# Turning the last batch's q with a transposing transfer, in a new order of all units

## The chip, the cores and the metric

The kernel runs on one core of one Trainium2 chip. The metric is the device time of one execution in microseconds (us); lower is better. The core has five engines with an instruction queue each: TensorE (PE; its weight loads are listed as PEld), VectorE (DVE), ScalarE (ACT), GpSimd (POOL) and SyncE (SP), which here only starts transfers. Sixteen DMA engines serve all queues.

## The reference

The inputs are q, k and v of shape (4 batches, 8 heads, 768 tokens, 64), a small matrix `sort_net` of 8 x 8 for each batch and head, and the weights of a gated layer. All are float32.

```
for _ in range(5):                       # P = sort_net, over 8 blocks of 96 tokens
    P = exp(P - max(P)); P /= rowsum(P); P /= colsum(P)
k_sorted, v_sorted = P @ k_blocks, P @ v_blocks           # blocks mixed by P
attn = softmax(q_block @ k_sorted_block.T / 8)            # 96 x 96 in each block
x = (attn @ v_sorted_block), heads side by side           # (4, 768, 512)

h = relu(x @ w_in);  u, v = h[:, :512], h[:, 512:]
v_n = (v - mean) / sqrt(var + 1e-6)
out = (u * (w_spatial @ v_n + b_spatial)) @ w_out         # (4, 768, 512)
```

## The kernel before

The kernel is written as units, small functions that each put a few instructions on one or two engines. The string `ORDER` (lines 18 to 51) names all units with their arguments, and the program calls them in that order; there is no scheduler behind it. Each engine works through its own instructions in the order in which the units issued them, and semaphores make it wait for what it reads and for the buffers it overwrites. So the order of the string decides everything. Most units that use TensorE begin with a number 0 to 3, the PSUM buffer (`ps0` to `ps3`, 4 KB per partition each) that takes the product; a letter A (ScalarE), D (VectorE) or P (GpSimd) names the engine that does the unit's copy or elementwise step. A PSUM buffer is free for the next unit when that copy has read it.

The units, with the line of their main instruction:

- Loads: `L:q:b`, `L:k:b`, `L:v:b` load one batch on GpSimd's queue, converting to bfloat16 (768 KB each); `L:wv`, `L:wu` are the halves of w_in, `L:wsa`, `L:wsb` those of w_spatial, `L:wo` is w_out. `LH` loads half of batch 0's q as float32 on SP, `QC` converts it. The tiles of q, k and v, of w_spatial and of the output come from one pool of eight, so a load can wait for a tile to come free.
- `DM` are filler products of a zero tile (L226), `SK` is one round of normalizing `sort_net` on ScalarE and VectorE, `PR` (L256) spreads the result over partitions, `P0`, `PC` and `PD` make from it the mixing matrices `pd` (batch 0 on VectorE, the others on GpSimd).
- q: `QT` and `QQ` turn the q of one or two pairs of heads, so that the head dimension lies on partitions, by products with the identity (L314: 12 or 24 of them), and copy the result from PSUM into `qT`. There are four pairs of heads in a batch.
- k: `KT` (L383) mixes the blocks of k and turns them in one product, and copies them into `kt_all` (six slots).
- v: batch 0 by `VT` (L383) and `VB` (L401); other batches by `VM` (L410) into the tile `vm`, which `VC` (L423, four transfers each on SP) rearranges into `vb`.
- Attention for a pair of heads and half of the blocks: `SC` (L442) makes the scores and ScalarE their exponentials (L447, five slots); `AT` (L488) multiplies them with v, and VectorE divides by the sums (L495, L496), giving `x_sb`.
- `XT` (L518) turns x by products with the identity in batches 0 and 1. In batches 2 and 3 `XD` does it with a transposing transfer on SP (L506, `dma_start_transpose`, 96 x 2048 elements).
- `VP` (L554; two tiles of 128 tokens, or one) makes the second half of h and `UP` (L597) the first. `ST` (L571, L572), `LN` and `LA` (L583) normalize the second half. `WW` (L531) turns w_spatial.
- `SP` (L609) multiplies with w_spatial, and VectorE adds the bias, giving `z` (L615, three tiles); `GT` (L626) multiplies z and u on VectorE or GpSimd, giving `gt`; `OP` (L635) multiplies with w_out. With a last argument 2 an `OP` does its 512 columns in two halves, 16 products of 256 columns in place of 8 of 512. `OE` (L115, L117) copies the result out of PSUM, `OS` stores it from SP's queue.
- The last batch uses finer units after a branch on a flag (`CK`, `CF`, `LF`): `SH`, `GH`, `OH` (L685), `OI` and `OJ` (L697), the last of which stores on SP's (S) or ScalarE's (A) queue.

In the old order every q is turned on TensorE: four `QT` in batch 0 and two `QQ` in each of batches 1, 2 and 3. Two units that the old order doesn't call are in the code all the same. `QP` (line 357) copies one pair of heads of q within SBUF into a tile `qp`, so that the two heads of a pair lie side by side. `QX` (line 368) turns all of it in one transposing transfer on SP:

```
        nc.sync.dma_start_transpose(
            out=q_tile(b)[:, lo * S:hi * S].rearrange("p (x c) -> p x c", c=128),
            in_=st["qp", b][:, lo:hi].rearrange("p k g h d -> p (k g h d)"),
        )
```

Of the kernel before, what the change touches and what calls it, by code (L numbers as in the profile page):

```python
# [15 lines left out]


ORDER = """
IV:0 CO S0 SK:0 SK:1 LH:S:0 L:q:0:4:8 L:k:0:0:8 L:v:0:0:8 SK:2 IV:2 ID MA L:v:1:0:8 MC QC:A:1 SK:3 L:k:1:0:8 MB QC:A:0
DM:0:6:512 L:q:1:0:8 DM:2:6:512 DM:1:6:512 QT:3:A:0:1 SK:4 QT:2:A:0:3 DM:0:6:512 DM:3:6:512 L:wv QT:1:A:0:0 QT:2:A:0:2  # L20
PR:0 P0:0:2 L:wu P0:6:8 P0:2:4 DM:3:6:512 P0:4:6 PC:D KT:1:D:0:1 PD:1:4:8 KT:3:A:0:0 L:wsb L:wsa KT:0:D:0:3 KT:2:A:0:2
IV:1 L:v:2:0:8 VT:1:A:0:0 VT:3:D:0:1 PD:1:0:4 SC:0:0:0:0 SC:2:0:0:1 VB:1:D:0:0 L:k:2:0:8 VB:3:D:0:1 SC:0:0:1:0
VT:1:A:0:2 AT:2:0:0:0 VT:3:A:0:3 PD:2:4:8 AT:0:0:1:0 L:q:2:0:8 VM:1:A:1:0 VB:2:D:0:2 SC:3:0:1:1 XT:0:D:0:0:0
AT:1:0:0:1 SC:2:0:2:0 VM:3:A:1:3 VB:0:D:0:3 PD:2:0:4 SC:1:0:2:1 AT:2:0:2:0 KT:3:D:1:1 KT:0:D:1:2 SC:1:0:3:0 VM:2:A:1:1
SC:3:0:3:1 AT:1:0:1:1 KT:2:A:1:3 KT:0:A:1:0 AT:3:0:3:0 VM:1:A:1:2 PD:3:4:8 QQ:2:D:1:0 XT:3:D:0:1:0 L:k:3:0:8
AT:0:0:3:1 XT:1:A:0:0:2 QQ:2:A:1:2 AT:3:0:2:1 VP:1:A:0:0:1 XT:0:D:0:1:2 ST:0:1 VP:2:D:0:2 ST:0:0 SC:0:1:1:1 SC:3:1:2:1
L:q:3:0:8 VC:1:4:8 VP:1:D:0:4:5 SC:2:1:3:1 ST:0:4 ST:0:5 SC:3:1:3:0 VP:0:A:0:3 SC:2:1:0:1 ST:0:2 UP:1:A:0:1:1
AT:0:1:1:1 L:v:3:0:8 SC:3:1:0:0 ST:0:3 UP:2:A:0:0:0 AT:0:1:3:1 AT:1:1:2:1 LN:0:0:6 UP:3:A:0:0:1 AT:0:1:0:1 LA:0:5
WW:2:A:0 WW:1:D:4 XT:3:A:1:1:2 UP:0:A:0:1:0 LA:0:2 VC:1:0:4 AT:2:1:0:0 VM:1:A:2:1 BI WW:3:D:2 SC:0:1:2:0 VM:2:A:2:2
XT:1:D:1:1:0 LA:0:0 BH LA:0:4 LA:0:1 LA:0:3 VM:3:A:2:0 SC:0:1:1:0 VP:1:A:1:4:5 AT:2:1:3:0 AT:0:1:1:0 ST:1:5 SP:3:0:2  # L30
AT:0:1:2:0 L:wo SP:1:0:0 VM:2:D:2:3 SP:0:0:1 VC:2:4:8 XT:3:D:1:0:2 XT:1:A:1:0:0 VC:2:0:4 QQ:2:D:2:0 KT:0:A:2:1
KT:3:D:2:0 GT:D:0:0 QQ:1:D:2:2 KT:2:A:2:2 KT:0:A:2:3 PD:3:0:4 GT:P:0:2 VP:3:A:1:0:1 SC:1:2:0:1 SC:2:2:0:0 SP:0:0:3
ST:1:4 SC:3:2:2:1 SC:1:2:1:1 ST:1:1 VP:2:A:1:2:3 KT:3:D:3:2 QQ:0:D:3:0 ST:1:2 SC:1:2:3:0 UP:2:A:1:1:0 AT:0:2:0:1
GT:P:0:3 KT:3:A:3:0 ST:1:3 QQ:1:D:3:2 SC:0:2:3:1 AT:2:2:2:1 UP:3:D:1:0:1 VM:1:A:3:3 UP:0:A:1:0:0 AT:2:2:3:1
UP:3:A:1:1:1 GT:P:0:1 ST:1:0 LN:1:0:6 AT:2:2:1:1 AT:0:2:3:0 XD:2:1 LA:1:4 OP:1:0:0:2 AT:2:2:0:0 OE:A:0:0 OP:0:0:2:2
SC:2:2:2:0 LA:1:2 LA:1:5 OE:D:0:2 SC:1:2:1:0 LA:1:1 LA:1:0 LA:1:3 OP:3:0:4:2 AT:1:2:1:0 AT:0:2:2:0 SP:2:1:2 VM:0:D:3:1
VM:1:D:3:0 OE:A:0:4 VP:3:D:2:4:5 KT:0:A:3:1 KT:2:D:3:3 SP:1:1:3 VM:0:A:3:2 GT:D:1:3 OS:0:0 ST:2:4 SP:3:1:1 SC:2:3:3:1
SC:1:3:1:1 XD:2:0 OS:0:2 GT:D:1:2 ST:2:5 SP:0:1:0 VC:3:4:8 SC:3:3:2:1 SC:2:3:0:1 UP:1:D:2:1:0 GT:D:1:1 VC:3:0:4
VP:3:A:2:2:3 AT:1:3:3:1 GT:P:1:0 VP:2:A:2:0:1 ST:2:3 AT:1:3:2:1 AT:3:3:1:1 UP:0:A:2:1:1 OP:1:1:0 ST:2:0 ST:2:1 ST:2:2
OE:A:1:0 AT:2:3:0:1 LN:2:0:6 LA:2:1 UP:0:D:2:0:0 SC:1:3:0:0 LA:2:3 SC:3:3:1:0 LA:2:2 LA:2:5 LA:2:0 OP:2:1:4 AT:1:3:0:0  # L40
AT:3:3:1:0 XD:3:1 OE:A:1:4 OP:0:1:2 LA:2:4 SC:1:3:3:0 OE:D:1:2 SC:3:3:2:0 SP:2:2:2 AT:1:3:2:0 UP:0:A:2:0:1 AT:3:3:3:0
CK VP:2:A:3:4:5 GT:D:2:2 OS:1:2 SP:1:2:1 ST:3:5 OS:1:4 XD:3:0 SP:3:2:3 SP:2:2:0 ST:3:4 CF:3 GT:D:2:1 GT:P:2:3
UP:0:A:3:1:0 VP:2:D:3:2:3 VP:3:A:3:0:1 ST:3:0 ST:3:1 ST:3:2 UP:2:A:3:0:1 GT:P:2:0 LF OP:1:2:2 ST:3:3 OE:A:2:2 LN:3:0:6
OP:0:2:0 LA:3:4 LA:3:5 OS:2:2 OE:A:2:0 UP:3:D:3:1:1 LA:3:2 LA:3:0 OP:2:2:4 LA:3:3 OE:A:2:4 LA:3:1 OS:2:4 UP:0:A:3:0:0
SH:1:3:3:0 GH:P:3:3:0 SH:2:3:0:0 GH:D:3:0:0 SH:0:3:1:0 SH:2:3:2:0 SH:3:3:1:1 GH:P:3:1:0 SH:1:3:0:1 GH:P:3:2:0 OS:1:0
GH:P:3:1:1 SH:2:3:3:1 SH:3:3:2:1 OS:2:0 GH:P:3:0:1 GH:D:3:2:1 GH:D:3:3:1 OS:0:4 IF OH:1:3:2:0:512:0:4
OH:2:3:3:0:512:0:4 OH:0:3:4:0:256:0:4 OI:A:3:2:0:512 OI:A:3:3:0:512 OH:3:3:5:0:256:0:4 OI:D:3:4:0:256 OI:D:3:5:0:256
OJ:3:2:0:512:S OJ:3:3:0:512:S OJ:3:4:0:256:S OJ:3:5:0:256:A OH:2:3:5:256:512:0:4 OH:1:3:1:0:512:0:4
OH:3:3:4:256:512:0:4 OI:D:3:5:256:512 OI:A:3:1:0:512 OJ:3:5:256:512:S OI:A:3:4:256:512 OJ:3:4:256:512:S OJ:3:1:0:512:A
OH:2:3:0:0:512:0:4 OI:A:3:0:0:512 OJ:3:0:0:512:S  # L50
"""


# [773 lines left out]
```

## Time and profile before

| | |
|---|---|
| median of 3 runs | 156.73 us (156.33 to 156.81) |
| the profiled execution: time, span | 156.77 us, 155.0 us |
| PE busy | 148.5 us (96% of the span) |
| DVE busy | 120.3 us (78%) |
| ACT busy | 81.6 us (53%) |
| POOL busy | 36.8 us (24%) |
| DMA, share of 16 engines | software queue (POOL) 48.0%, hardware queue (SP) 25.4% |
| loaded from HBM, written to it | 24.78 MB, 6.29 MB |

The span runs from the first to the last instruction that the profiler saw; the execution's own time holds 1.77 us more. Busy shares are averages over stages. Of the chain of work that ended last 93% of the span are PE's. A line of the chain reads start, length, engine, line and count; a line of the timeline reads start, length, engine, line, what is written and read, count and, in brackets, the idle time ahead of it with what ended it.

### The profile page before, as it was taken

Reading aid. Unit: us, or ns where it says so; the run is one execution under the profiler, and the core shown is the slowest. Engines: PE = TensorE matmul, PEld = TensorE weight load, DVE = VectorE, ACT = ScalarE, POOL = GpSimd, SP = SyncE. Lnnn points to the kernel's source line nnn. Section 1 sums busy time; section 2 is a strip of 40 time slices with the busy share of each in tenths; the row PEclk is TensorE's granted clock in tenths of the full one; section 3 lists DMA queues with packets and bytes.
Section 4 is the critical chain, followed back from the end, with each engine's and each line's share of the span. In section 5 each row is a group of like instructions: output and inputs, shape, how many; then the busy total and the mean of one; then the engine's idle time right before and its main releaser. Section 6 shows DMA issues by size and latency. Waiting matters only on the chain.

```text
span 155.0 us, 4028 instructions
## 1 busy us (share of the span) xinstructions
PE 148.5 (96%) x1689; PEld 92.1 (59%) x1689; DVE 120.3 (78%) x261; ACT 81.6 (53%) x112; POOL 36.8 (24%) x43
## 2 busy tenths in 40 slices
...
GB/s 72 267 203 204 205 204 205 208 217 238 271 217 203 203 204 204 242 226 16 0 17 224 43 198 64 147 1 4 102 148 185 44 0 0 131 49 371 141 226 183
DMA packets 27653, 23.57 MB, mean 152 GB/s; under 512 B 7280, under 2 KB 24688, under 8 KB 27632
## 3 DMA queue, kind: packets, MB, share of 16 engines
q0 software_dynamic: 14352, 11.80, 48.0%
q1 hardware_dynamic: 12992, 11.10, 25.4%
...
q8 instruction: 14, 0.23, 0.6%
...
HBM read 24.78 MB, written 6.29 MB: 201 GB/s over the span
## 4 chain that ended last, share of the span: by engine, by line
PE 93%; ACT 3%; DVE 1%; issue 1%; DVEq 0%; ACTq 0%
PE ps L609 15%; PE ps L554 14%; PE ps L597 14%; PE ps L635 10%; PE ps L226 7%; PE ps L488 5%; PE ps L665 5%; PE ps L442 4%; PE ps L383 4%; PE ps L314 4%; PE ps L685 3%; PE ps L410 2%; PE ps L518 2%; PE ps L531 1%; PE ps L401 1%; ACT kt_all L115 1%
## 5 line engine op out<-in xcount | busy, mean ns | idle before, releaser
L447 ACT ACTIVATE ex_all<-ps 96x768 bf16<-96x768 f32 x32 | 24.8, 805 | 8.7 <-PE ps L442 8.6
L626 POOL TENSOR_TENSOR gt<-z,u_sb 128x768 bf16<-128x768 f32 x6 | 9.8, 1642 | 78.6 <-DVE z L615 61.3
L609 PE MATMUL ps<-wspT,v_sb 128*128 128x384 bf16 x144 | 25.1, 326 | 0.0
L597 PE MATMUL ps<-xT,w_in_sb 128*128 128x384 bf16 x128 | 23.5, 326 | 0.0
L554 PE MATMUL ps<-w_in_sb,xT 128*128 128x512 bf16 x96 | 22.9, 380 | 0.2 <-issue 0.2
L496 DVE TENSOR_TENSOR x_sb<-ps,rec_all 96x512 bf16<-96x512 f32 x32 | 22.0, 687 | 1.1
L609 PEld LDWEIGHTS <-v_sb 128*128 128x128 bf16 x144 | 13.5, 98 | 8.9
L571 DVE BATCH_NORM_STATS2 stats<-v_sb 128x6 f32<-128x512 bf16 x24 | 16.3, 678 | 2.0 <-ACT v_sb L121 1.5
L115 ACT COPY o_sb<-ps 128x1024 f32<-128x1024 f32 (+2 forms) x12 | 9.7, 816 | 15.2 <-PE ps L685 10.2
L635 PE MATMUL ps<-w_out_sb,gt 128*128 128x256 bf16 (+1 forms) x96 | 16.9, 326 | 0.0
L615 DVE TENSOR_TENSOR z<-ps,b_bc 128x768 f32<-128x768 f32 x12 | 11.4, 952 | 7.0 <-PE ps L609 6.8
L121 ACT ACTIVATE u_sb<-ps 128x768 bf16<-128x768 f32 x12 | 9.7, 810 | 13.1 <-PE ps L597 13.0
L597 PEld LDWEIGHTS <-w_in_sb 128*128 128x128 bf16 x128 | 11.6, 98 | 7.4
L554 PEld LDWEIGHTS <-xT 128*128 128x128 bf16 x96 | 8.6, 98 | 9.7 <-issue 0.7
L121 ACT ACTIVATE v_sb<-ps 128x1024 bf16<-128x1024 f32 (+1 forms) x9 | 8.8, 976 | 9.1 <-PE ps L554 9.1
L488 PEld LDWEIGHTS <-ex_all 96*128 96x128 bf16 x256 | 10.6, 97 | 3.7 <-issue 0.6
L488 PE MATMUL ps<-vb,ex_all 96*128 96x65 bf16 x256 | 12.2, 193 | 0.5 <-issue 0.5
L635 PEld LDWEIGHTS <-gt 128*128 128x128 bf16 x96 | 9.0, 98 | 5.5
L226 PE MATMUL ps<-warm 128*128 128x512 bf16 x36 | 10.7, 461 | 1.3 <-DVE warm L201 1.3
L115 ACT CAST kt_all<-ps 128x768 bf16<-128x768 f32 x9 | 6.9, 800 | 6.5 <-PE ps L383 6.5
L442 PE MATMUL ps<-qT,kt_all 64*128 64x96 bf16 x256 | 9.3, 204 | 0.4 <-DVE kt_all L117 0.4
L495 DVE RECIPROCAL rec_all<-ps 96x8 f32<-96x8 f32 x32 | 6.3, 196 | 4.3 <-PE ps L488 4.0
...
## 6 DMA issues: line engine op xcount, KB each, us to landing
...
k_in<-in_k_dram POOLq DMA_DIRECT2D x4, 768.0 KB, 23.2
v_in<-in_v_dram POOLq DMA_DIRECT2D x4, 768.0 KB, 22.3
vb<-vm SPq DMA_DIRECT2D x24, 99.0 KB, 5.8
q_in<-in_q_dram POOLq DMA_DIRECT2D x3, 768.0 KB, 29.8
...
q<-in_q_dram SPq DMA_DIRECT2D x1, 768.0 KB, 4.6
```

The source lines that it names most:

```text
L115: nc.scalar.copy(out=out, in_=in_)
L121: nc.scalar.activation(out=out, in_=in_, func=AF.Relu)
L226: nc.tensor.matmul(t[:, 0, 0:int(w)], lhsT=warm[:, 0:128], rhs=warm[:, 0:int(w)], start=True, stop=True)
L442: nc.tensor.matmul(t[:, hh, 0:HW].rearrange("p (g x) -> p g x", g=G)[:, :, ii * TB:(ii + 1) * TB], lhsT=kT[rows, i * BLK:i * BLK + 128], r ...
L447: nc.scalar.activation(out=e_tile(b, hp, ih).rearrange("p h (x g) -> p h x g", g=G), in_=t[0:BLK, :, 0:HW].rearrange("p h (g x) -> p h x g ...
L488: nc.tensor.matmul(t[:, hh, ii * VW:ii * VW + D + 1], lhsT=e[:, c:c + 128], rhs=vb[b % 2][:, ih * NI + ii, 2 * hp + hh, 0:D + 1], start=Tr ...
L496: nc.vector.tensor_mul(out=x_sb[:, hp].rearrange("p i (h d) -> p h i d", h=2), in0=tv[:, :, :, 0:D], in1=_raw_ap(rec, 0, [rec.ap[0], [NI, ...
L554: nc.tensor.matmul(t[:, x, :], lhsT=st["xT", b][:, n // 3, kc, (n % 3) * 128:(n % 3 + 1) * 128], rhs=w_in_sb[:, kc, DH:DFF], start=(kc == ...
L571: nc.vector.bn_stats(out=stats, in_=st["v_sb", b, n])
L597: nc.tensor.matmul(t[:, x, 0:HW], lhsT=w_in_sb[:, kc, mc * 128:(mc + 1) * 128], rhs=st["xT", b][:, ih, kc, :], start=(kc == 0), stop=(kc = ...
L609: nc.tensor.matmul(t[:, x, 0:HW], lhsT=st["v_sb", b, n][:, mc * 128:(mc + 1) * 128], rhs=wspT[:, 3 * x:3 * x + 3, n, :], start=(n == 0), s ...
L635: nc.tensor.matmul(t[:, x, c:c + w], lhsT=st["gt", b, mc][:, (n0 + x) * 128:(n0 + x + 1) * 128], rhs=w_out_sb[:, mc, c:c + w], start=(mc = ...
```

## The change

The string `ORDER` is replaced; no function changes. The new string differs in four ways:

- Batch 3 has no `QQ`. Four `QP` (three on ScalarE, one on VectorE) and one `QX:3:0:4` take their place: 128 x 3072 elements in one transposing transfer on SP, behind the `VC` of batch 2 and ahead of the first `XD`.
- All other units are the same in number, but nearly all stand at other places, use other PSUM buffers, and in part copy on another engine. Batch 0's first loads are v, k, half of q (before: half of q, k, v), those of batch 1 v, q, k (before: v, k, q), those of batch 3 q, v, k. The order holds 62 changes between products of different shape (64 columns, 64 rows, full), where the old one holds 65.
- All nine `OP` of batches 0 to 2 are done in two halves; before, only the three of batch 0.
- In the tail the products, copies and stores come in another order: the last `OH` has 256 columns and is copied by VectorE (before: 512 columns, ScalarE), and four of its eight stores go out on ScalarE's queue (before: two of eight). The last two entries of the list are both stores, `OJ:3:4:0:256:A` ahead of `OJ:3:5:256:512:S`, exchanged against the order in which their copies stand.

```diff
 ORDER = """
-IV:0 CO S0 SK:0 SK:1 LH:S:0 L:q:0:4:8 L:k:0:0:8 L:v:0:0:8 SK:2 IV:2 ID MA L:v:1:0:8 MC QC:A:1 SK:3 L:k:1:0:8 MB QC:A:0
-DM:0:6:512 L:q:1:0:8 DM:2:6:512 DM:1:6:512 QT:3:A:0:1 SK:4 QT:2:A:0:3 DM:0:6:512 DM:3:6:512 L:wv QT:1:A:0:0 QT:2:A:0:2
-PR:0 P0:0:2 L:wu P0:6:8 P0:2:4 DM:3:6:512 P0:4:6 PC:D KT:1:D:0:1 PD:1:4:8 KT:3:A:0:0 L:wsb L:wsa KT:0:D:0:3 KT:2:A:0:2
-IV:1 L:v:2:0:8 VT:1:A:0:0 VT:3:D:0:1 PD:1:0:4 SC:0:0:0:0 SC:2:0:0:1 VB:1:D:0:0 L:k:2:0:8 VB:3:D:0:1 SC:0:0:1:0
-VT:1:A:0:2 AT:2:0:0:0 VT:3:A:0:3 PD:2:4:8 AT:0:0:1:0 L:q:2:0:8 VM:1:A:1:0 VB:2:D:0:2 SC:3:0:1:1 XT:0:D:0:0:0
-AT:1:0:0:1 SC:2:0:2:0 VM:3:A:1:3 VB:0:D:0:3 PD:2:0:4 SC:1:0:2:1 AT:2:0:2:0 KT:3:D:1:1 KT:0:D:1:2 SC:1:0:3:0 VM:2:A:1:1
-SC:3:0:3:1 AT:1:0:1:1 KT:2:A:1:3 KT:0:A:1:0 AT:3:0:3:0 VM:1:A:1:2 PD:3:4:8 QQ:2:D:1:0 XT:3:D:0:1:0 L:k:3:0:8
-AT:0:0:3:1 XT:1:A:0:0:2 QQ:2:A:1:2 AT:3:0:2:1 VP:1:A:0:0:1 XT:0:D:0:1:2 ST:0:1 VP:2:D:0:2 ST:0:0 SC:0:1:1:1 SC:3:1:2:1
-L:q:3:0:8 VC:1:4:8 VP:1:D:0:4:5 SC:2:1:3:1 ST:0:4 ST:0:5 SC:3:1:3:0 VP:0:A:0:3 SC:2:1:0:1 ST:0:2 UP:1:A:0:1:1
-AT:0:1:1:1 L:v:3:0:8 SC:3:1:0:0 ST:0:3 UP:2:A:0:0:0 AT:0:1:3:1 AT:1:1:2:1 LN:0:0:6 UP:3:A:0:0:1 AT:0:1:0:1 LA:0:5
-WW:2:A:0 WW:1:D:4 XT:3:A:1:1:2 UP:0:A:0:1:0 LA:0:2 VC:1:0:4 AT:2:1:0:0 VM:1:A:2:1 BI WW:3:D:2 SC:0:1:2:0 VM:2:A:2:2
-XT:1:D:1:1:0 LA:0:0 BH LA:0:4 LA:0:1 LA:0:3 VM:3:A:2:0 SC:0:1:1:0 VP:1:A:1:4:5 AT:2:1:3:0 AT:0:1:1:0 ST:1:5 SP:3:0:2
-AT:0:1:2:0 L:wo SP:1:0:0 VM:2:D:2:3 SP:0:0:1 VC:2:4:8 XT:3:D:1:0:2 XT:1:A:1:0:0 VC:2:0:4 QQ:2:D:2:0 KT:0:A:2:1
-KT:3:D:2:0 GT:D:0:0 QQ:1:D:2:2 KT:2:A:2:2 KT:0:A:2:3 PD:3:0:4 GT:P:0:2 VP:3:A:1:0:1 SC:1:2:0:1 SC:2:2:0:0 SP:0:0:3
-ST:1:4 SC:3:2:2:1 SC:1:2:1:1 ST:1:1 VP:2:A:1:2:3 KT:3:D:3:2 QQ:0:D:3:0 ST:1:2 SC:1:2:3:0 UP:2:A:1:1:0 AT:0:2:0:1
-GT:P:0:3 KT:3:A:3:0 ST:1:3 QQ:1:D:3:2 SC:0:2:3:1 AT:2:2:2:1 UP:3:D:1:0:1 VM:1:A:3:3 UP:0:A:1:0:0 AT:2:2:3:1
-UP:3:A:1:1:1 GT:P:0:1 ST:1:0 LN:1:0:6 AT:2:2:1:1 AT:0:2:3:0 XD:2:1 LA:1:4 OP:1:0:0:2 AT:2:2:0:0 OE:A:0:0 OP:0:0:2:2
-SC:2:2:2:0 LA:1:2 LA:1:5 OE:D:0:2 SC:1:2:1:0 LA:1:1 LA:1:0 LA:1:3 OP:3:0:4:2 AT:1:2:1:0 AT:0:2:2:0 SP:2:1:2 VM:0:D:3:1
-VM:1:D:3:0 OE:A:0:4 VP:3:D:2:4:5 KT:0:A:3:1 KT:2:D:3:3 SP:1:1:3 VM:0:A:3:2 GT:D:1:3 OS:0:0 ST:2:4 SP:3:1:1 SC:2:3:3:1
-SC:1:3:1:1 XD:2:0 OS:0:2 GT:D:1:2 ST:2:5 SP:0:1:0 VC:3:4:8 SC:3:3:2:1 SC:2:3:0:1 UP:1:D:2:1:0 GT:D:1:1 VC:3:0:4
-VP:3:A:2:2:3 AT:1:3:3:1 GT:P:1:0 VP:2:A:2:0:1 ST:2:3 AT:1:3:2:1 AT:3:3:1:1 UP:0:A:2:1:1 OP:1:1:0 ST:2:0 ST:2:1 ST:2:2
-OE:A:1:0 AT:2:3:0:1 LN:2:0:6 LA:2:1 UP:0:D:2:0:0 SC:1:3:0:0 LA:2:3 SC:3:3:1:0 LA:2:2 LA:2:5 LA:2:0 OP:2:1:4 AT:1:3:0:0
-AT:3:3:1:0 XD:3:1 OE:A:1:4 OP:0:1:2 LA:2:4 SC:1:3:3:0 OE:D:1:2 SC:3:3:2:0 SP:2:2:2 AT:1:3:2:0 UP:0:A:2:0:1 AT:3:3:3:0
-CK VP:2:A:3:4:5 GT:D:2:2 OS:1:2 SP:1:2:1 ST:3:5 OS:1:4 XD:3:0 SP:3:2:3 SP:2:2:0 ST:3:4 CF:3 GT:D:2:1 GT:P:2:3
-UP:0:A:3:1:0 VP:2:D:3:2:3 VP:3:A:3:0:1 ST:3:0 ST:3:1 ST:3:2 UP:2:A:3:0:1 GT:P:2:0 LF OP:1:2:2 ST:3:3 OE:A:2:2 LN:3:0:6
-OP:0:2:0 LA:3:4 LA:3:5 OS:2:2 OE:A:2:0 UP:3:D:3:1:1 LA:3:2 LA:3:0 OP:2:2:4 LA:3:3 OE:A:2:4 LA:3:1 OS:2:4 UP:0:A:3:0:0
-SH:1:3:3:0 GH:P:3:3:0 SH:2:3:0:0 GH:D:3:0:0 SH:0:3:1:0 SH:2:3:2:0 SH:3:3:1:1 GH:P:3:1:0 SH:1:3:0:1 GH:P:3:2:0 OS:1:0
-GH:P:3:1:1 SH:2:3:3:1 SH:3:3:2:1 OS:2:0 GH:P:3:0:1 GH:D:3:2:1 GH:D:3:3:1 OS:0:4 IF OH:1:3:2:0:512:0:4
-OH:2:3:3:0:512:0:4 OH:0:3:4:0:256:0:4 OI:A:3:2:0:512 OI:A:3:3:0:512 OH:3:3:5:0:256:0:4 OI:D:3:4:0:256 OI:D:3:5:0:256
-OJ:3:2:0:512:S OJ:3:3:0:512:S OJ:3:4:0:256:S OJ:3:5:0:256:A OH:2:3:5:256:512:0:4 OH:1:3:1:0:512:0:4
-OH:3:3:4:256:512:0:4 OI:D:3:5:256:512 OI:A:3:1:0:512 OJ:3:5:256:512:S OI:A:3:4:256:512 OJ:3:4:256:512:S OJ:3:1:0:512:A
-OH:2:3:0:0:512:0:4 OI:A:3:0:0:512 OJ:3:0:0:512:S
+S0 CO SK:0 BH LH:S:0 IV:2 L:v:0:0:8 SK:1 SK:2 ID MA L:k:0:0:8 L:q:0:4:8 DM:3:6:512 DM:0:6:512 L:v:1:0:8 L:q:1:0:8
+QC:A:0 SK:3 QC:A:1 MB SK:4 DM:2:6:512 DM:1:6:512 MC QT:2:D:0:1 DM:1:6:512 DM:3:6:512 PR:1 L:k:1:0:8 QT:2:A:0:0 P0:0:2
+L:wv L:wsb P0:4:6 P0:6:8 IV:0 P0:2:4 PC:D VT:0:A:0:0 KT:3:D:0:0 L:wu PD:1:0:4 VT:2:A:0:1 L:v:2:0:8 KT:1:A:0:3
+KT:0:D:0:2 SC:2:0:0:1 VB:3:D:0:0 PD:1:4:8 KT:1:A:0:1 QT:0:D:0:2 IV:1 QT:2:A:0:3 VB:3:D:0:1 SC:0:0:1:0 VT:1:D:0:3
+VT:2:A:0:2 L:wsa L:q:2:0:8 SC:3:0:0:0 PD:3:0:4 PD:3:4:8 AT:0:0:0:1 L:k:2:0:8 VB:1:D:0:3 SC:2:0:1:1 AT:3:0:0:0
+VM:0:A:1:0 VB:1:D:0:2 SC:2:0:2:0 AT:3:0:1:0 SC:0:0:3:0 AT:1:0:2:0 SC:2:0:2:1 AT:3:0:1:1 VM:0:A:1:2 AT:2:0:3:0
+XT:1:A:0:0:0 VM:0:D:1:3 QQ:3:D:1:2 SC:1:0:3:1 VM:2:D:1:1 XT:0:A:0:1:0 KT:1:A:1:2 L:q:3:0:8 AT:3:0:3:1 L:wo VC:1:4:8
+KT:0:A:1:1 AT:2:0:2:1 KT:1:A:1:0 VC:1:0:4 QQ:3:D:1:0 KT:0:A:1:3 PD:2:0:4 XT:2:D:0:0:2 XT:1:D:0:1:2 PD:2:4:8 SC:3:1:0:1
+SC:0:1:2:0 VP:2:D:0:0:1 ST:0:0 SC:0:1:1:1 SC:1:1:3:1 ST:0:1 VP:3:A:0:4:5 VP:2:A:0:2 VP:1:A:0:3 ST:0:5 L:v:3:0:8
+WW:2:A:4 ST:0:3 SC:3:1:3:0 AT:0:1:0:1 UP:1:A:0:1:0 ST:0:2 ST:0:4 AT:0:1:3:1 UP:2:A:0:0:0 LN:0:0:6 AT:3:1:2:0
+UP:1:A:0:0:1 LA:0:2 AT:0:1:1:1 LA:0:3 LA:0:1 LA:0:0 SC:2:1:2:1 UP:3:A:0:1:1 AT:0:1:2:1 LA:0:4 VM:1:A:2:0 WW:2:D:0
+VM:3:A:2:1 LA:0:5 L:k:3:0:8 SC:0:1:1:0 WW:1:D:2 VM:3:A:2:3 XT:2:D:1:1:0 VM:0:D:2:2 SC:1:1:0:0 AT:3:1:3:0 QQ:2:D:2:2 BI
+AT:0:1:1:0 SP:1:0:1 XT:2:A:1:1:2 AT:3:1:0:0 SP:0:0:3 VC:2:4:8 GT:P:0:3 XT:1:A:1:0:2 XT:2:D:1:0:0 SP:3:0:0 KT:1:A:2:2
+KT:0:A:2:0 VC:2:0:4 KT:2:D:2:3 QQ:3:A:2:0 KT:1:A:2:1 SC:2:2:2:1 VP:0:A:1:0:1 GT:D:0:0 QP:A:3:3 ST:1:1 ST:1:0
+VP:3:A:1:4:5 ST:1:4 ST:1:5 GT:P:0:1 SC:1:2:0:0 SC:2:2:1:1 SP:0:0:2 SC:3:2:0:1 SC:1:2:3:1 VP:2:A:1:2:3 QP:A:3:1
+GT:D:0:2 AT:1:2:0:0 UP:3:A:1:0:1 ST:1:2 AT:0:2:3:1 UP:2:A:1:0:0 ST:1:3 LN:1:0:6 AT:3:2:1:1 LA:1:3 OP:0:0:0:2 OE:A:0:0
+LA:1:5 AT:3:2:0:1 VM:1:A:3:2 QP:A:3:2 UP:2:A:1:1:0 QP:D:3:0 LA:1:2 LA:1:1 VM:3:D:3:0 OP:0:0:2:2 QX:3:0:4 LA:1:0
+AT:1:2:2:1 OE:A:0:2 KT:3:A:3:1 KT:2:D:3:2 LA:1:4 XD:2:1 SC:1:2:2:0 SC:0:2:1:0 SC:3:2:3:0 OP:2:0:4:2 VM:0:D:3:1
+AT:3:2:2:0 SP:1:1:3 OE:A:0:4 AT:0:2:1:0 AT:2:2:3:0 SP:3:1:2 UP:1:A:1:1:1 KT:2:D:3:3 GT:D:1:2 XD:2:0 KT:0:A:3:0
+VM:3:A:3:3 VC:3:4:8 SP:1:1:1 SC:2:3:1:1 SC:0:3:2:1 VP:3:D:2:4:5 SC:0:3:3:1 SC:2:3:1:0 ST:2:4 OS:0:4 VP:1:A:2:0:1
+GT:P:1:3 AT:0:3:1:1 AT:3:3:2:1 GT:P:1:1 SP:2:1:0 ST:2:5 AT:1:3:3:1 UP:3:A:2:0:0 UP:0:D:2:1:1 GT:D:1:0 SC:2:3:0:1
+SC:1:3:3:0 VP:3:A:2:2:3 AT:1:3:0:1 UP:2:A:2:1:0 ST:2:0 ST:2:1 VC:3:0:4 SC:0:3:2:0 ST:2:3 ST:2:2 SC:3:3:0:0 XD:3:1
+OP:1:1:0:2 AT:2:3:1:0 OE:A:1:0 OS:0:0 LN:2:0:6 AT:0:3:2:0 LA:2:5 UP:3:A:2:0:1 LA:2:4 OP:1:1:2:2 LA:2:0 OE:A:1:2 LA:2:3
+LA:2:2 AT:3:3:0:0 LA:2:1 VP:0:A:3:4:5 AT:3:3:3:0 XD:3:0 OP:1:1:4:2 CK ST:3:4 SP:2:2:3 SP:0:2:2 SP:3:2:0 GT:P:2:2
+VP:0:A:3:2:3 GT:D:2:3 VP:2:A:3:0:1 ST:3:3 SP:3:2:1 OE:A:1:4 ST:3:0 GT:P:2:1 CF:2 OS:0:2 OS:1:2 GT:P:2:0 UP:0:A:3:0:1
+ST:3:5 ST:3:2 UP:1:D:3:1:0 LF ST:3:1 LN:3:0:6 LA:3:2 OS:1:0 UP:2:D:3:1:1 OP:0:2:2:2 UP:3:D:3:0:0 LA:3:4 OP:1:2:0:2
+OE:A:2:2 LA:3:0 LA:3:3 OP:2:2:4:2 OE:A:2:0 OE:A:2:4 LA:3:1 LA:3:5 SH:0:3:2:0 SH:3:3:3:0 GH:P:3:3:0 SH:2:3:0:0
+GH:D:3:2:0 SH:0:3:1:0 GH:P:3:0:0 SH:3:3:1:1 SH:2:3:2:1 OS:2:4 GH:P:3:1:0 SH:1:3:3:1 OS:2:0 GH:D:3:1:1 SH:3:3:0:1
+OS:1:4 GH:D:3:3:1 OS:2:2 GH:P:3:0:1 GH:P:3:2:1 IF OH:0:3:2:0:512:0:4 OI:A:3:2:0:512 OH:1:3:3:0:512:0:4
+OH:2:3:0:0:512:0:4 OI:D:3:0:0:512 OI:A:3:3:0:512 OH:0:3:1:0:512:0:4 OJ:3:2:0:512:S OJ:3:3:0:512:A OI:A:3:1:0:512
+OJ:3:0:0:512:S OH:1:3:4:256:512:0:4 OI:D:3:4:256:512 OH:3:3:5:0:256:0:4 OI:D:3:5:0:256 OJ:3:1:0:512:S OJ:3:4:256:512:A
+OH:2:3:5:256:512:0:4 OJ:3:5:0:256:A OI:D:3:5:256:512 OH:0:3:4:0:256:0:4 OI:D:3:4:0:256 OJ:3:4:0:256:A OJ:3:5:256:512:S
 """
```

## The prediction

> **What bounds the kernel now.** I read the page first (span, engine shares), then the windows (is TensorE ever idle?), then the chain of waits in order of time (what each kind of product costs), then the loads' time to landing, and last the evictions at the places where the new order is tight.
>
> ```profile
> span 155.0 us, 4028 instructions
> ```
>
> ```profile
> 12.00:34.00 22.00, 20.40 (x417) 15.20 (x416) 17.58 (x33) 17.65 (x24) 12.12 (x14) 1.00 1.28 206
> 34.00:151.00 117.00, 117.00 (x1199) 72.05 (x1195) 95.29 (x190) 57.24 (x77) 16.87 (x14) 1.00 0.63 138
> ```
>
> The windows give start:end, length, then busy us of PE, PEld, DVE, ACT and POOL, the granted clock, DMA share and GB/s. From 34 us to 151 us TensorE is busy for 117.00 of 117.00 us at a granted clock of 1.00: every microsecond of product taken off its list there comes off the end, and every new wait is added to it. Only between 12 and 34 us is it idle, for 1.6 us, and there the DMA engines are full (share 1.28).
>
> The chain in order of time gives start, length and count of each stretch that decided the end:
>
> ```profile
> 28.57 0.79 PE ps L314 x24
> ...
> 59.02 0.68 PE ps L518 x16
> 59.70 0.79 PE ps L314 x24
> 60.49 0.67 PE ps L383 x24
> 61.16 0.67 PE ps L314 x24
> 61.83 0.67 PE ps L383 x24
> 62.50 1.83 PE ps L554 x8
> 64.33 0.45 PE ps L442 x16
> ...
> 78.88 1.75 PE ps L635 x16
> ...
> 102.90 0.48 PE ps L488 x16
> 103.39 1.30 PE ps L597 x8
> 104.69 1.73 PE ps L635 x8
> ...
> 118.47 5.85 PE ps L609 x36
> ```
>
> Twenty-four q transposes (L314, one QQ) cost 0.67 us behind the mixing products of k (L383), which use the same 64 columns, and 0.79 behind a product of another shape (L518). So a change between the three shapes (64 columns: QT, QQ, KT, VT; 64 rows: SC; full: the rest) costs about 0.10 us. Counted over the two lists there are 65 such changes before and 62 after. The other prices: XT 0.34 (L518 x8), KT, VT and QT 0.335 (x12), VP pair 1.73 (1.83 less the change), SC 0.225 (L442 x8), AT 0.24 (L488 x8), UP 1.30, OP 1.73, SP 1.95 (5.85 / 3); VM and WW I estimate at 0.33 and 0.67, as a quarter of UP and as a QQ.
>
> **The change part by part.** *Work on TensorE.* Two QQ go: 2 x 0.67 = 1.34 us. Three shape changes go: 0.3 us. Six OP are done in halves (1.75 in place of 1.73): +0.12 us. Net -1.5 us, if nothing else moved.
>
> *The start, up to PR.*
>
> ```profile
> 11.97 0.36 PE L256 MATMUL ps<-p_t,spread 32*128 32x32 bf16 x8
> 12.27 1.47 PE L226 MATMUL ps<-warm 128*128 128x512 bf16 x6
> ```
>
> The old list has 30 filler products and four QT ahead of PR (L256), the new one 36 and one: +1.4 for six fillers, -1.2 for three QT with a change (0.79 for two of them). I take PR's start as unchanged, 0.2 us either way.
>
> *The first loads* set the next 16 us. That queue works in order and is full, so a load should land where the same sum of bytes landed before.
>
> ```profile
> 2.20 0.89 POOL L171 DMA_DIRECT2D k_in<-in_k_dram  x1
> ...
> 6.35 0.89 POOL L171 DMA_DIRECT2D q_in<-in_q_dram  x1
> ...
> 16.95 0.92 POOL L171 DMA_DIRECT2D v_in<-in_v_dram  x1
> ```
>
> ```profile
> k_in<-in_k_dram POOLq DMA_DIRECT2D x1, 768.0 KB, 9.3
> q_in<-in_q_dram POOLq DMA_DIRECT2D x1, 768.0 KB, 21.4
> v_in<-in_v_dram POOLq DMA_DIRECT2D x1, 768.0 KB, 29.3
> ```
>
> ```profile
> 15.41 0.86 PE L383 MATMUL ps<-pd,v_in 128*64 128x128 bf16 x24 [0.21 <-DMA v_in<-in_v_dram]
> ```
>
> Issue plus time to landing: k of batch 0 at 11.5, q of batch 1 at 27.75, v of batch 2 at 46.25; v of batch 0, the load behind that first k, at 15.4, where TensorE resumes (so 3.9 us for a load). In the new order v comes first, then k, then the half q: k of batch 0 lands halfway between 11.5 and 15.4, at 13.4, just when the list wants it (PR's end at 12.3, a QT and a VT with two changes: 13.2). K of batch 1 has the place of q of batch 1: 27.75. Block wsa has that of v of batch 2: 46.25. Q of batch 2 follows it: 50.1.
>
> The old stretch from PR to the QQ at 28.57 took 16.6 us, waits and all. Up to the first KT of batch 1 the new list has four KT and six fillers fewer, three QT, one XT and one QQ more, and two changes fewer: -1.34 - 1.4 + 1.0 + 0.34 + 0.67 - 0.2 = -0.9. With the old sum of waits (the new ones are VT behind the last quarter of pd, and SC behind a KT copy that queues behind pd and prep on VectorE) that KT would start at 27.7; k lands at 27.75. I take 27.8.
>
> *From there to the end* the lists can be subtracted again. The old one took 151.39 - 28.57 = 122.8 us from that QQ to the last eviction (its row is below). The new rest has four KT more (+1.34), three QQ fewer (-2.01), one XT fewer (-0.34), the six split OP (+0.12) and 40 changes as before: -0.9. Without new waits the products end at 27.8 + 122.8 - 0.9 = 149.7.
>
> *New waits, by place.* SC:1:2:2:0 takes the PSUM bank of AT:1:2:2:1 with only two KT between (0.67 + 0.10).
>
> ```profile
> 79.60 0.19 DVE L495 RECIPROCAL rec_all<-ps 96x8 f32<-96x8 f32 x1
> 79.83 0.69 DVE L496 TENSOR_TENSOR x_sb<-ps,rec_all 96x512 bf16<-96x512 f32 x1
> ```
>
> The bank is free 0.92 us (79.60 to 80.52) and two handoffs, which I put at 0.05 each, after AT: 0.25. The KT copy queued behind it on VectorE holds OP:2:0:4:2 for some 0.15 more. Two similar reuses (SC:1:1:0:0, SC:2:2:2:1) I put at 0.1 each. Late in batch 2, OP:0:2:2:2 waits for two products of gate and z on GpSimd, both behind the last SP:
>
> ```profile
> 124.35 0.96 DVE L615 TENSOR_TENSOR z<-ps,b_bc 128x768 f32<-128x768 f32 x1 [0.99 <-PE ps L609]
> ```
>
> ```profile
> 126.27 1.64 DVE L626 TENSOR_TENSOR gt<-z,u_sb 128x768 bf16<-128x768 f32 x1
> ```
>
> ```profile
> 125.45 1.64 POOL L626 TENSOR_TENSOR gt<-z,u_sb 128x768 bf16<-128x768 f32 x1 [0.28 <-DVE z L615]
> ```
>
> Counted from SP's end (118.47 + 5.85 = 124.32 in the old run) GpSimd starts 1.13 us later and needs 2 x 1.64, in all 4.4; TensorE meanwhile has CF (0.1) and three UP, 4.0: a wait of 0.4. In the old run VectorE's own gate product, started beside GpSimd's, took 1.64 us, against 0.96 for the z sum of the same size; GpSimd's stayed at 1.64. The Trainium skill, "SBUF — State Buffer", on the port pair shared by VectorE and GpSimd, calls it an exclusive lock: whoever starts first holds it for the whole instruction, the other is blocked. The trace agrees (1.64 on VectorE, GpSimd not slowed). By that rule a two-input VectorE instruction that started first would make the 0.4 up to 1.3; the new list has none between that z and those two products, so the sum keeps 0.4. All new waits: 0.25 + 0.15 + 0.2 + 0.4 = 1.0. Products end at 150.7.
>
> *The transposing transfer* (QX) is not in the trace of before. Nearest:
>
> ```profile
> xT<-x_sb SPq DMA_TRANSPOSE x4, 3.8
> ```
>
> ```profile
> vb<-vm SPq DMA_DIRECT2D x8, 99.0 KB, 2.8
> ```
>
> It moves 128 x 3072 elements, twice the 96 x 2048 of an XD: 3.8 us at best, 7.6 if it scales; I take 7.6. It goes out once the four QP copies are through (three on ScalarE, busy 57.24 of 117 us, one on VectorE; I put them at 0.8 each, as other 128x768 copies, beside other work), by the list at about 77, and lands by 85. The first SC of batch 3 stands behind 12 KT, 18 AT, 3 QQ, 6 XT, 16 SC, six VP pairs, 3 WW, 8 UP, 8 VM, 7 SP, 3 OP and 33 changes, 63.6 us after that KT: 91.8 with the waits, 7 us to spare. Behind QX on SP's queue stand XD:2:1 (lands by 89, wanted at 92), XD:2:0 and VC:3. VC:3 is tightest: by the same sums the last VM copy ends at 90.9, its fourth transfer is issued at 92.7 and lands 2.8 later, 95.5; AT wants it at 96.3. So QX costs nothing, with 0.8 us of cover; each microsecond beyond is one of the end. On VectorE two copies go and one comes.
>
> *The tail.* The last eviction, 128x512 on ScalarE, becomes 128x256 on VectorE.
>
> ```profile
> 149.22 0.42 DVE L117 COPY o_sb<-ps 128x256 f32<-128x256 f32 x1
> ```
>
> ```profile
> 151.39 0.58 ACT L115 COPY o_sb<-ps 128x512 f32<-128x512 f32 x1 [0.44 <-PE ps L685]
> ```
>
> From the last product to the span's end it was 155.0 - 151.4 = 3.6; 0.16 less is 3.5. The last two stores go out on different queues, so their exchange in the list moves nothing.
>
> *Sum.* Span 150.7 + 3.5 = 154.2. The profiled execution took 156.77 for its span of 155.0, 1.77 outside: 155.97, **156.0 us**. The median of the runs is 156.73, so the profile stands for it.
>
> **The rivals.** *No new wait* (0.15): VectorE and GpSimd are ahead at all four places: 156.0 - 1.0 = 155.0. For it: no idle time after 34 us in the old run. Against: the bank reuse and the gate chain are sums of single rows without slack.
>
> *Handoffs eat the gain* (0.23): more places like the four, VectorE being busy 95.29 of 117 us and the new list giving ScalarE more copies. Another 0.7 us gives 156.7, no change.
>
> *Slower by the loads* (0.12): the queue doesn't follow the bytes. If k of batch 0, wanted at 13.2, lands where v did (15.4), the first KT waits 2.0 us more than summed, and all behind it: 158.0. It decides from about 14.6 on. Wsa (wanted at 46.3 by the list) and q of batch 2 (50.1) have no slack either. Against: the bytes ahead of each are known.
>
> *Slower by SP's queue* (0.08): QX is far slower than its size says, and XD:2:0 and VC:3 come late behind it. VC:3 2.8 us late is 2.0 beyond its cover: 158.0; slower than before from 1.6 late.
>
> That the change doesn't do what it says is no case: the list has no QQ of batch 3, and that batch's SC read what QX wrote.
>
> **How the numbers follow.** The forecast has 0.42. About 0.3% (0.47 us) is what a measurement here can tell from no change. Faster by more than that (under 156.26): no new wait, and five sixths of the forecast, 0.50. Within it: the rest of the forecast and most of the handoff case, 0.28. Slower (over 157.2): both slow cases and a remnant, 0.22. The range goes from no new wait, 155.0, to handoffs with PR and a load 0.2 late each, 157.1.
>
> **What would show it.** Right: L314 x144 in place of x192; the first KT of batch 1 near 27.8 with k's landing as releaser; TensorE idle 0.2 to 0.4 before L442 near 80 us and before L635 near 131; last product near 150.7. Wrong: idle beyond 1 us before the first L383 of k, L442 waiting for qT, L488 for vb near 96 us, or a last product past 151.4.

## The result, and the profile after

The changed kernel takes 157.06 us (median of 8 runs, 156.79 to 157.25), the kernel before 156.56 us (8 runs beside it, 156.33 to 156.82). The ratio is 1.0029, 95% interval 1.0018 to 1.0040: the change makes the kernel 0.5 us slower. The forecast was 156.0 us. The profiled execution after took 157.07 us for a span of 155.2 us (before 156.77 and 155.0).

The transposing transfer does what was meant. The group of q transposes has gone from x192 to x144, and QX is issued at 77.33 and lands 7.5 us later, where "at about 77, lands by 85" was forecast; no product waits for it.

```profile
L314 PE MATMUL ps<-ident,q_in 128*64 128x128 bf16 x144 | 5.3, 221 | 0.5 <-ACT q_in L115 0.5
```

```profile
77.33 3.72 SPq L370 DMA_TRANSPOSE qT<-qp  x1
```

```profile
qT<-qp SPq DMA_TRANSPOSE x1, 7.5
```

The windows (the same stretches as before) show where TensorE is no longer full: 116.32 of 117.00 us from 34 to 151, where it was 117.00.

```profile
12.00:34.00 22.00, 20.54 (x459) 16.15 (x459) 18.82 (x35) 18.84 (x25) 12.04 (x14) 1.00 1.28 207
34.00:151.00 117.00, 116.32 (x1183) 75.59 (x1182) 87.92 (x183) 62.07 (x83) 18.07 (x14) 1.00 0.69 144
```

TensorE's timeline gives the places, first of the kernel before, then of the kernel after:

```profile
31.46 0.60 PE L554 MATMUL ps<-w_in_sb,xT 128*128 128x512 bf16 x2
...
130.41 3.62 PE L635 MATMUL ps<-w_out_sb,gt 128*128 128x512 bf16 x16
...
138.19 7.96 PE L665 MATMUL ps<-wspT,v_sb 128*128 128x512 bf16 x48
```

```profile
28.29 0.53 PE L383 MATMUL ps<-pd,k_in 128*64 128x128 bf16 x12 [0.19 <-ACT ex_all L447]
...
31.36 0.97 PE L518 MATMUL ps<-ident,x_sb 96*128 96x96 bf16 x16
...
78.94 0.86 PE L383 MATMUL ps<-pd,k_in 128*64 128x128 bf16 x24
80.03 0.89 PE L442 MATMUL ps<-qT,kt_all 64*128 64x96 bf16 x24 [0.23 <-DVE x_sb L496]
80.89 1.91 PE L635 MATMUL ps<-w_out_sb,gt 128*128 128x256 bf16 x16
...
127.13 4.08 PE L597 MATMUL ps<-xT,w_in_sb 128*128 128x384 bf16 x24
131.61 1.92 PE L635 MATMUL ps<-w_out_sb,gt 128*128 128x256 bf16 x16 [0.40 <-POOL gt L626]
...
138.16 7.96 PE L665 MATMUL ps<-wspT,v_sb 128*128 128x512 bf16 x48
```

The two lists can be compared at places where both have done the same units (but for batch 3's QQ), and there are three good ones:

- Ahead of the old first VP (31.46) the old list has done what the new one has done between its two XT, at 31.36 + 0.97 / 2 = 31.8: the new order is **0.35 us behind**.
- Where the old OP of batch 2 starts (130.41), the new list is behind two of the three UP that start at 127.13, so at 127.13 + 2 x 1.30 = 129.73: **0.68 ahead**. In between it gained 1.03 us, of the 1.34 of the QQ and the 0.2 of two changes of shape that it has fewer there.
- At the first SH (L665) it is 138.16 against 138.19: **level**. The 0.65 us went mostly ahead of OP:0:2:2:2.

From there on the products are equal; the last one ends at 151.3 in both. The chain shows the wait ahead of that OP: z of the last SP, then two products of gate and z on GpSimd in a row.

```profile
127.10 0.11 PE ps L725
127.21 0.96 DVE z L615
...
128.31 1.40 POOL gt L626
...
129.91 1.65 POOL gt L626
131.56 0.05 issue
131.61 1.92 PE ps L635 x16
...
151.33 0.02 issue
151.36 0.42 DVE o_sb L117
```

So product for product nothing was won, and the time behind the products grew: 157.07 - 151.33 = 5.74 us, before 156.77 - 151.37 = 5.40, though the last copy got shorter.

### The profile page after: what moved, and what is told of

Same layout as the page of the kernel before. It is cut to its first block, busy times and chain, and to the rows that moved or that the text cites. A ratio compares the mean times of both kernels' runs of the same rounds, so it can differ in the third digit from the quotient of the medians.

```text
span 155.2 us, 4033 instructions
## 1 busy us (share of the span) xinstructions
PE 147.4 (95%) x1689; PEld 96.0 (62%) x1689; DVE 115.4 (74%) x258; ACT 85.4 (55%) x116; POOL 38.8 (25%) x44
## 4 chain that ended last, share of the span: by engine, by line
PE 82%; DMA 7%; POOL 3%; DVE 2%; ACT 2%; issue 1%; POOLq 0%; ACTq 0%
PE ps L609 15%; PE ps L554 14%; PE ps L597 11%; PE ps L635 10%; DMA k_in<-in_k_dram 7%; PE ps L488 5%; PE ps L442 5%; PE ps L665 5%; PE ps L383 4%; PE ps L685 3%; PE ps L314 2%; PE ps L410 2%; POOL gt L626 2%; PE ps L518 2%; ACT ex_all L447 2%; PE ps L531 1%
## 5 line engine op out<-in xcount | busy, mean ns | idle before, releaser
L626 POOL TENSOR_TENSOR gt<-z,u_sb 128x768 bf16<-128x768 f32 x7 | 11.4, 1640 | 81.8 <-DVE z L615 52.5
L609 PE MATMUL ps<-wspT,v_sb 128*128 128x384 bf16 x144 | 25.1, 326 | 0.0
L597 PE MATMUL ps<-xT,w_in_sb 128*128 128x384 bf16 x128 | 23.0, 326 | 0.0
L554 PE MATMUL ps<-w_in_sb,xT 128*128 128x512 bf16 x96 | 22.3, 380 | 0.0
L115 ACT COPY o_sb<-ps 128x1024 f32<-128x1024 f32 (+1 forms) x12 | 10.9, 905 | 15.2 <-PE ps L685 9.1
L609 PEld LDWEIGHTS <-v_sb 128*128 128x128 bf16 x144 | 13.6, 98 | 8.5
L635 PE MATMUL ps<-w_out_sb,gt 128*128 128x256 bf16 x144 | 17.0, 273 | 0.4 <-POOL gt L626 0.4
L121 ACT ACTIVATE v_sb<-ps 128x1024 bf16<-128x1024 f32 (+1 forms) x11 | 10.3, 948 | 12.3 <-PE ps L554 12.3
L635 PEld LDWEIGHTS <-gt 128*128 128x128 bf16 x144 | 13.7, 98 | 2.8 <-POOL gt L626 0.8
L226 PE MATMUL ps<-warm 128*128 128x512 bf16 x36 | 9.8, 435 | 1.3 <-DVE warm L201 1.3
L115 ACT CAST kt_all<-ps 128x768 bf16<-128x768 f32 x11 | 8.7, 801 | 2.2 <-PE ps L383 2.2
L442 PEld LDWEIGHTS <-kt_all 64*128 64x128 bf16 x256 | 6.4, 94 | 5.4 <-issue 3.3
```

Source lines behind the costliest of these rows:

```text
L115: nc.scalar.copy(out=out, in_=in_)
L121: nc.scalar.activation(out=out, in_=in_, func=AF.Relu)
L442: nc.tensor.matmul(t[:, hh, 0:HW].rearrange("p (g x) -> p g x", g=G)[:, :, ii * TB:(ii + 1) * TB], lhsT=kT[rows, i * BLK:i * BLK + 128], r ...
L554: nc.tensor.matmul(t[:, x, :], lhsT=st["xT", b][:, n // 3, kc, (n % 3) * 128:(n % 3 + 1) * 128], rhs=w_in_sb[:, kc, DH:DFF], start=(kc == ...
L597: nc.tensor.matmul(t[:, x, 0:HW], lhsT=w_in_sb[:, kc, mc * 128:(mc + 1) * 128], rhs=st["xT", b][:, ih, kc, :], start=(kc == 0), stop=(kc = ...
L609: nc.tensor.matmul(t[:, x, 0:HW], lhsT=st["v_sb", b, n][:, mc * 128:(mc + 1) * 128], rhs=wspT[:, 3 * x:3 * x + 3, n, :], start=(n == 0), s ...
```

## The experiments

All times are medians; ratios are to the kernel before, run beside them, with the 95% interval. "The end" is the time from the first product of the tail (L685) to the end of the execution.

**The transfer alone, in the old order** (transfer_alone, transfer_early, transfer_cover).

```diff
 # transfer_alone: before, with
-QQ:0:D:3:0
+QP:D:3:0 QP:D:3:1
-QQ:1:D:3:2
+QP:D:3:2 QP:D:3:3 QX:3:0:4
```

> The old order with only the part that the change is named for: each of batch 3's two QQ becomes two QP copies on VectorE at the same place, and QX follows the second pair on SP's queue. No other unit moves. If the transfer itself is worth what the forecast says and the new order eats it, this kernel is 1.34 us faster than before (two QQ of 0.67 us, both between products of other shapes, so no change of shape goes with them): 155.2 us, 0.991 of before. If the transfer is what fails (late qT, or SP's queue late behind it), this kernel is no faster than before, 156.6 us or more, and the scores of batch 3 or AT wait for a transfer.

Measured 157.25 us, ratio 1.0041 (1.0027 to 1.0056): slower than before, by neither of the two mechanisms that were expected. q came in time. Part of the loss is an end that is 0.43 us longer, as in every kernel with the transfer (under "The end"). The rest is on TensorE, whose timeline shows two waits at the very places where the QQ had stood, 1.38 us for the 1.34 removed:

```profile
70.19 1.46 PE L597 MATMUL ps<-xT,w_in_sb 128*128 128x384 bf16 x8 [0.38 <-ACT v_sb L121]
...
73.36 0.34 PE L442 MATMUL ps<-qT,kt_all 64*128 64x96 bf16 x8 [1.00 <-DVE x_sb L496]
```

Each QQ had been the work that ran while another engine emptied the PSUM buffer of the product behind it. Two more kernels take this apart: the copies moved out of the way, and then other buffers as well.

```diff
 # transfer_early: before without the two QQ, and
-SC:2:2:0:0 SP:0:0:3
+SC:2:2:0:0 QP:D:3:0 QP:D:3:1 QP:D:3:2 QP:D:3:3 SP:0:0:3 QX:3:0:4
 # transfer_cover: that, and
-UP:2:A:1:1:0 AT:0:2:0:1
+UP:0:A:1:1:0 AT:1:2:0:1
 ...
-SC:0:2:3:1 AT:2:2:2:1 UP:3:D:1:0:1 VM:1:A:3:3
+SC:2:2:3:1 AT:0:2:2:1 UP:1:D:1:0:1 VM:3:A:3:3
```

> The old order with the transfer in place of the two QQ, as in transfer_alone, but the four QP copies go to VectorE ahead of z of SP:0:0:3, where it is idle for 2.85 us in the old trace (64.1 to 66.9), and QX follows at once. The PSUM buffers stay as they are. In transfer_alone the two places where a QQ had stood became waits: UP for the buffer that VP's relu empties (0.38 us) and SC for the buffer that VectorE's division empties (1.00 us, with two QP copies ahead of that division). If the lost cover alone makes these waits, they stay at 0.4 and about 0.7 and the kernel takes about 156.3 us; if VectorE's queue made the second one, it goes to 0.2 or less and the kernel takes about 155.8 us.

Measured 156.79 us, 1.0009 (1.0000 to 1.0017). The waits are 0.38 and 0.56: the lost cover makes most of them, two copies in VectorE's queue made 0.44. The 0.4 us that are left of the 1.34 go into the longer end.

```profile
70.15 1.46 PE L597 MATMUL ps<-xT,w_in_sb 128*128 128x384 bf16 x8 [0.38 <-ACT v_sb L121]
...
72.87 0.34 PE L442 MATMUL ps<-qT,kt_all 64*128 64x96 bf16 x8 [0.56 <-DVE x_sb L496]
```

> As transfer_early, and six units behind the two places use another PSUM buffer (UP 0 for 2, AT 1 for 2, SC 2 for 0, AT 0 for 2, UP 1 for 3, VM 3 for 1), so that each buffer has been free for some time when it is written. If the QQ were only cover for the copies that empty PSUM, TensorE now has no wait there and the whole 1.34 us of the two QQ shows: 155.3 us, 0.991 of before. If the transfer costs in another way (SP's queue, late x of batch 2), the kernel stays above 156 us without a wait at these places.

Measured **155.71 us, 0.9944 (0.9931 to 0.9958)**: faster than both kernels. No product waits there any more:

```profile
69.52 1.47 PE L597 MATMUL ps<-xT,w_in_sb 128*128 128x384 bf16 x8
...
71.62 0.34 PE L442 MATMUL ps<-qT,kt_all 64*128 64x96 bf16 x8
```

Its products end 1.3 to 1.5 us earlier than those of the old kernel (149.87; 151.37 and, in a second trace, 151.13), as the price of the QQ says, but the execution only 0.9 to 1.0 us earlier. The missing 0.4 is taken up under "The end".

**Pieces of the old order in the new one** (old_head, old_head_mended, old_tail). Each takes all units up to a place where both lists are level, or from there on, from the old list.

```diff
 # old_head: lines up to the old AT:3:0:2:1, then the rest of the new order, with
-XT:1:D:0:1:2 SC:3:1:0:1 SC:0:1:2:0
+XT:0:D:0:1:2 SC:1:1:0:1 SC:3:1:2:0
 # old_head_mended: the same, q of batch 2 loaded ahead of k, and
-XT:1:D:0:1:2 SC:3:1:0:1 SC:0:1:2:0 VP:2:D:0:0:1
+VP:0:D:0:0:1 XT:2:D:0:1:2 SC:1:1:0:1 SC:3:1:2:0
 # old_tail: the changed kernel, from IF on the old list
```

> The changed kernel, but with the units of the old order up to the last AT ahead of the first VP (31.46 us in the old trace). At that place the two orders have done exactly the same work on TensorE, the new one 0.36 us later (31.82). The three units behind the seam use other PSUM banks. If the new order's start is a real loss, the 0.36 us come back: 156.7 us, against 157.06 for the changed kernel. If time lost early is absorbed by waits later, it stays at 157.06.

> As old_head (the changed kernel with the old order up to the first VP), with its two seams mended: VP goes ahead of the XT that waited 1.03 us for x, in another buffer, and q of batch 2 is loaded ahead of k, since the new order wants it first (a wait of 2.63 us in old_head). If the new order's start is a real loss of 0.36 us and nothing else waits, 156.7 us against 157.06. If the old start only looks better because it leaves work on VectorE and ScalarE for later, 157.0 us or more, with waits in the 20 us behind the seam.

Measured 161.68 us, 1.0307 (1.0268 to 1.0347), and mended 158.03 us, 1.0089 (1.0076 to 1.0103), where 156.7 was the expectation. In the first the seam itself cost 1.03 us (XT for VectorE) and 2.63 us (q of batch 2, which the old loads bring later). In the second the first VP starts early (31.78), and the rest waits behind it, 0.53 us for VectorE's relu and 0.35 for an exponential:

```profile
35.09 0.61 PE L442 MATMUL ps<-qT,kt_all 64*128 64x96 bf16 x16 [0.53 <-DVE v_sb L123]
36.05 3.61 PE L554 MATMUL ps<-w_in_sb,xT 128*128 128x512 bf16 x15 [0.35 <-ACT ex_all L447]
```

So the old start is not 0.35 us better that one could graft. The wait for VectorE's relu suggests that part of its lead is work left on VectorE; how much is the seam's own doing can't be read from this.

> The changed kernel with the products, copies and stores of the old tail (all behind the branch). The last product ends at 151.3 us in both traces, and the span goes on for 3.6 us in the old and 3.9 in the new one. If the new stores cost that, 0.25 to 0.35 us come back: 156.75 us. If the tail's length comes from something else, it stays at 157.06.

Measured 157.84 us, 1.0082 (1.0069 to 1.0096). The old tail's products wait for gates that the new order brings in another sequence, so the graft lost more than it could show. But behind its last product it takes 5.85 us (157.85 - 152.00), no less than the 5.74 of the new tail, and from the landing of the last store to the end of the span both take 1.39 us: the new stores were not the cause.

**The gate chain** (gate_swap).

```diff
-GT:P:2:1 CF:2 OS:0:2 OS:1:2 GT:P:2:0
+GT:P:2:0 CF:2 OS:0:2 OS:1:2 GT:P:2:1
```

> The changed kernel with two of GpSimd's gate products of batch 2 exchanged: GT:P:2:0, whose z is there early, ahead of GT:P:2:1, whose z comes last. Then only one product of 1.64 us is left behind the last z, 2.8 us behind SP's end, while TensorE has 4.0 us of work before OP:0:2:2:2. If that chain costs what the trace shows (OP starts 0.58 us later than the three UP before it explain), the kernel takes 156.5 us. If OP waits for something else as well, less than 0.3 us comes back.

Measured 156.60 us, 0.9995 (0.9984 to 1.0007), 0.46 us less than the changed kernel, and the OP starts at 130.98 in place of 131.61. The chain that the prediction priced at 0.4 costs 0.6. GpSimd's line shows the middle product done early and only one left behind the last z:

```profile
122.80 2.20 POOL L626 TENSOR_TENSOR gt<-z,u_sb 128x768 bf16<-128x768 f32 x1 [0.27 <-DVE z L615]
128.19 1.64 POOL L626 TENSOR_TENSOR gt<-z,u_sb 128x768 bf16<-128x768 f32 x1 [3.18 <-DVE z L615]
```

The first of them took 2.20 us, not 1.64: VectorE's own product of gate and z had started before it.

```profile
122.55 0.95 DVE L626 TENSOR_TENSOR gt<-z,u_sb 128x768 bf16<-128x768 f32 x1
```

This is the other side of the lock that the Trainium skill, "SBUF — State Buffer", "SBUF: two separate sides", describes on the port pair shared by VectorE and GpSimd (whoever starts first holds it): here VectorE kept its 0.95 us and GpSimd, which started 0.70 us before VectorE's end, lost 0.56.

**ScalarE or VectorE in the head** (scalar_extra, scalar_less).

```diff
 # scalar_extra: a copy of warm (128 x 512) on ScalarE, result unused
-VM:0:A:1:0
+XA VM:0:A:1:0
 # scalar_less
-VM:0:A:1:0
+VM:0:D:1:0
 ...
-XT:0:A:0:1:0
+XT:0:D:0:1:0
```

> The changed kernel with one more copy on ScalarE (128 x 512 bf16 into a tile that nobody reads) ahead of the copy of batch 1's first VM, near 21 us. ScalarE is busy for 18.84 of the 22 us from 12 to 34 in the changed kernel. If ScalarE sets the pace of this stretch, the first VP and the end come later by the time that the copy takes, about 0.4 to 0.5 us: 157.5 us. If TensorE's waits there come from VectorE or from the order of the products, they come less than 0.15 us later.

> The changed kernel with two of ScalarE's copies in the head given to VectorE (batch 1's first VM near 21 us, the XT near 28 us). Three products in the changed kernel's head wait 0.19 to 0.28 us each for an exponential on ScalarE. If ScalarE alone sets the pace there, the first VP comes 0.3 us or more earlier (32.4 us, 156.7). If both engines are full (VectorE is without a gap from 20.3 to 30.6 us as well), the waits only change their name and the first VP comes no earlier than 32.7.

With the extra copy (0.61 us) the first VP starts at 32.76 in place of 32.71. The median is 157.44 us, 1.0050 (1.0037 to 1.0063), above the changed kernel's; its trace does not show why, the profiled execution took 157.02. With two copies given to VectorE, where they take 0.94 and 0.55 us, the first VP starts at 34.29, 1.6 us later, and the kernel takes 158.12 us, 1.0089 (1.0073 to 1.0104). The windows of the new head, of the changed kernel and then of the one before, fit this: VectorE is busy for 10.21 of 10.60 us, before for 9.68, ScalarE for 9.11 and 9.24.

```profile
20.30:30.90 10.60, 9.81 (x216) 7.51 (x215) 10.21 (x20) 9.11 (x13) 5.16 (x6) 1.00 1.28 207
```

```profile
20.30:30.90 10.60, 9.98 (x226) 7.90 (x225) 9.68 (x19) 9.24 (x13) 6.26 (x7) 1.00 1.29 206
```

The waits in the new head name ScalarE's exponentials, but VectorE is the engine without slack: 0.61 us more on ScalarE moved the first VP by 0.05 us, 1.5 us more on VectorE by 1.6.

**The change without the transfer** (qq_back): no QP and no QX, and

```diff
-UP:1:A:1:1:1 KT:2:D:3:3 ...
+UP:1:A:1:1:1 QQ:0:D:3:0 QQ:2:D:3:2 KT:1:D:3:3 ...
```

> The changed kernel without the transfer: QP and QX are out and two QQ of batch 3 stand behind the UP near 88 us, with six units on other PSUM buffers. They add 2 x 0.67 us and some 0.2 us of waits for a buffer. If the transfer gains in the new order what it removes, 158.5 us. If it has a fixed price of 0.4 us at the end, this kernel is saved that price: 158.1 us, with an end of 10.7 us from the first L685. If the transfer is worth nothing there, 157.06.

Measured 158.26 us, 1.0106 (1.0092 to 1.0121). The products end 1.76 us later than in the changed kernel (153.09), the execution 1.2, since its end is shorter (10.62 us in place of 11.11). So the transfer gains in the new order about what it gains in the old one, and the reordering without it costs about 1.7 us, some 0.4 of which are waits and changes of shape around the QQ put back here.

**The end.** Every kernel with the transfer ends later behind its products than its tail says. What does this go by?

```diff
 # spare_transfer: before, with a transfer of q of batch 3 into a tile that nobody reads
-SP:0:0:3
+SP:0:0:3 XS        # dma_start_transpose on SP, 128 x 3072
 # spare_half: 128 x 1536;  spare_plain: dma_start, not turned, 128 x 3072
 # cover_split: transfer_cover, with
-QX:3:0:4
+QX:3:0:2 QX:3:2:4
 # cover_bias: transfer_cover, and bias_alone: before, with b_bc's load (BI)
-        nc.sync.dma_start(
+        nc.gpsimd.dma_start(
```

> The old kernel once more, for its trace. From the start of the tail's first product (L685) to the end of the execution the first trace of it has 10.78 us, and three kernels with the very same tail and the transposing transfer have 11.21 each. If the old kernel's end is shorter because it has no such transfer, this trace shows 10.8 again; if the first trace was a chance, it shows 11.2 with products that end about 0.4 us earlier.

> The old kernel with all its QQ, and beside them one transposing transfer of q of batch 3 (128 x 3072 elements, as QX) into a tile that nobody reads, at the place where transfer_cover has QX. No product and no copy changes. If a transfer of this kind costs the execution a fixed 0.4 us at its end, this kernel takes 157.1 us and its end is 11.2 us long; if not, it takes 156.7 us with the end that the old kernel has.

> As spare_transfer, with half of the transfer (128 x 1536 elements). The whole one made the time from the first L685 to the end 11.21 us in place of 10.78, with no product touched. If that price goes by the size, the end is 11.0 us long and the kernel 0.2 us slower than before; if any transfer of this kind costs it, 11.2 us and 0.4.

> As spare_transfer, but the same 768 KB are copied within SBUF by an ordinary transfer, not turned. If the price at the end belongs to the turning (its 3104 more packets), the end is 10.8 us long as in the old kernel, and the time is that of before; if it belongs to the bytes or to one more transfer on SP, 11.2 us and 0.4 us slower.

> transfer_cover with its QX in two halves, one behind the other on SP. If the price at the end comes from one large transfer, the end goes from 11.21 to 10.8 us and the kernel to 155.3; if it goes by the sum of what is turned, nothing changes (155.7, 0.994 of before).

> transfer_cover with the load of b_bc (one transfer of 384 KB) on GpSimd's queue in place of SP's, where GpSimd is idle. SP then starts as many transfers as in the old kernel. The price of 0.43 us at the end went neither by size nor by turning nor by halves; if it goes by the number of transfers on SP's queue, the time from the first L685 to the end falls from 11.21 to 10.8 us and the kernel takes 155.3 us. If it goes by the number of transfers in all, or by something else, nothing changes: 155.7.

> The old kernel with the load of b_bc on GpSimd's queue: one transfer fewer on SP's. If each transfer on SP costs 0.43 us at the end, the end goes from 10.78 to 10.35 us and the kernel to 156.2. If there is a step between the old kernel's number and one more, or the price is not SP's, nothing changes: 156.6.

The rows of L685 in the old kernel's second trace and in spare_transfer are the same within 0.1 us, and the executions took 156.55 and 156.88:

```profile
145.77 5.36 PE L685 MATMUL ps<-w_out_sb,gt 128*128 128x512 bf16 x31
```

```profile
145.67 5.36 PE L685 MATMUL ps<-w_out_sb,gt 128*128 128x512 bf16 x31
```

In this table the transfers started by SP's and ScalarE's queues are counted from the list of DMA issues; the times are of the profiled execution.

| kernel | tail | transfers | first L685 | time | the end | last store landed to end of span |
|---|---|---|---|---|---|---|
| before | old | 48 | 145.99 | 156.77 | 10.78 | 0.97 |
| before_again | old | 48 | 145.77 | 156.55 | 10.78 | 0.97 |
| spare_transfer | old | 49 | 145.67 | 156.88 | 11.21 | 1.39 |
| spare_half | old | 49 | 145.75 | 156.97 | 11.22 | 1.39 |
| spare_plain | old | 49 | 146.00 | 157.20 | 11.20 | 1.39 |
| transfer_cover | old | 49 | 144.50 | 155.71 | 11.21 | 1.39 |
| cover_split | old | 50 | 144.53 | 155.67 | 11.14 | 1.33 |
| cover_bias | old | 48 | 157.25 | 168.08 | 10.83 | 0.98 |
| bias_alone | old | 47 | 158.07 | 168.92 | 10.85 | 1.03 |
| after | new | 49 | 145.96 | 157.07 | 11.11 | 1.39 |
| gate_swap | new | 49 | 145.32 | 156.34 | 11.02 | 1.39 |
| qq_back | new | 48 | 147.73 | 158.35 | 10.62 | 0.97 |

The ratios agree: spare_transfer 1.0028 (1.0017 to 1.0039), spare_half 1.0030 (1.0017 to 1.0042), spare_plain 1.0027 (1.0015 to 1.0040), cover_split 0.9944 (0.9930 to 0.9957). The 0.43 us don't go by size or by turning, and they are gone when b_bc moves to GpSimd's queue. The last column shows where they lie: between the landing of the last store and the end of the span.

There SP waits for the program's semaphores (the counters by which engines and transfers tell that they are done) with twelve wait instructions, one behind the other (L822). They start about 0.06 us apart even when their semaphores have long been set. The transfers of SP's and ScalarE's queues signal eight of these semaphores in turn. After 48 transfers, six rounds of eight, the last store signals the last of the eight that SP asks for, and one wait instruction is left when it has landed. After 49 the last store signals the first of the eight: SP stops there until it has landed, and has all eight to go through. The rows give, from the landing on, the wait instructions (number; shortest, median and longest in ns; start of the first and the last), first of the kernel before, then of spare_transfer:

```profile
L822 SPq EVENT_SEMAPHORE  x1: 28/28/28, 154.0 to 154.0; - x1
```

```profile
L822 SPq EVENT_SEMAPHORE  x8: 27/28/28, 153.7 to 154.1; - x8
```

Seven more waits of 0.06 us are the 0.42 us between 0.97 and 1.39. The other two counts fit: after 50 transfers seven wait instructions are left (1.33 us), after 47 two (1.03 us). So the price goes by the place of the last store's semaphore in the sequence, not by a limit at 48; counts other than 47 to 50 were not run.

cover_bias and bias_alone took 168.31 and 169.41 us for another reason, which their expectations missed. GpSimd was idle, but its queue was full of loads, and b_bc landed 28.7 us after its issue (row below; on SP's queue 9.1), so that the first z waited 10.6 us for it. Behind that wait TensorE was slow for some time: its granted clock in cover_bias was 0.50 from 66 to 70 us and 0.85 from 70 to 75, where transfer_cover has 1.00, and 12 products of L609 took 4.02 us in place of 2.1.

```profile
b_bc<-in_moe_b_spatial_dram POOLq DMA_DIRECT2D x1, 384.0 KB, 28.7
```

**A shorter tail for the fastest kernel** (cover_tail).

```diff
-OH:3:3:4:256:512:0:4 OI:D:3:5:256:512 ... OH:2:3:0:0:512:0:4 OI:A:3:0:0:512 OJ:3:0:0:512:S
+OI:D:3:5:256:512 ... OH:2:3:0:0:512:0:4 OI:A:3:0:0:512 ... OH:3:3:4:256:512:0:4 OI:D:3:4:256:512 ...
```

> transfer_cover with its last products in another order: the last one has 256 columns and is copied by VectorE (0.42 us in place of 0.58), and its store has 128 KB. The new tails measured 11.02 to 11.11 us from the first L685 to the end, the old ones with a transfer 11.21. If the last copy sets that, 0.16 us come off transfer_cover: 155.55 us. If the stores set it, nothing.

Measured 155.85 us, 0.9958 (0.9944 to 0.9971), and an end of 11.31 us: nothing gained. The last store is issued 0.14 us earlier (150.37 in place of 150.51), but it lands after 2.26 us in place of 2.01; why it takes longer is open.

## Why the prediction was wrong

Its sum was 155.97 for the profiled execution, which took 157.07. The 1.1 us lie in three of its steps:

- **The start, up to the first KT of batch 1: 0.5 us.** Forecast 27.8 with k's landing as releaser. k landed at 27.76, but the KT started at 28.29, behind an exponential. From PR to that KT it is 16.34 us, where the sum gave 15.7. The step that failed is "with the old sum of waits": the sum counted the units moved into this stretch (three QT, an XT, a QQ) as products and not as copies for ScalarE and VectorE, and VectorE has no room from 20.3 us on (busy for 10.21 of 10.60 us). That VectorE has no slack there is shown by scalar_less; which of the copies take it was not tried.
- **From there to the last product: 0.15 us** (123.05 against 122.9). The waits came at the forecast places, with their sizes too small. Near 80 us TensorE idles 0.23 ahead of SC, but the KT pair started at 78.94 and needs 0.79 with its change of shape, where SC came 1.09 later, and three SC that need 0.67 took 0.86: about 0.5 in place of 0.25 + 0.15. The gate chain cost 0.6 in place of 0.4. The bracket of 0.40 counts from the end of the three UP's row (127.13 + 4.08), which is 0.18 behind the 3 x 1.30 that they need. The two reuses at 0.1 each didn't show as idle time; PR's start (11.95) and the first loads (k of batch 0 by 13.4) came as forecast.
- **The end: 0.47 us** (5.74 against 3.5 + 1.77). The copy of 256 columns is worth what was said: with 48 transfers the new tail's end is 10.62 where the old one's is 10.78, with 49 it is 11.02 to 11.11 where the old one's is 11.20 to 11.22. What was missing is the 0.42 us that SP's last waits take longer with the 49th transfer. The prediction costed QX by its landing and by what stands behind it on SP's queue, and had no place for a price at the end of the execution.

The handoff rival (156.7, "no change") named the mechanism of the first two; no rival named the third. Both slow rivals, by the loads and by SP's queue, did not come: k of batch 0 landed at 13.38 and its first KT started at 13.43, 0.2 behind the 13.2 of the list, and no product waited for QX or what stands behind it. That the 157.06 lies inside the stated range is luck: its upper end stood for handoffs with PR and a load late, and both came in time.

The transfer was rightly priced (1.34 us, shown by transfer_cover), and so was its cover on SP. What the sum had wrong about it is shown by transfer_alone: a product that goes is worth its time only if it wasn't the cover under which another engine empties a PSUM buffer. The forecast looked for such places in the new order where it found a buffer reused at once, and took the rest of the time as a list of products.

What stays open: why scalar_extra's runs are slower than its trace says, why cover_tail's last store takes longer, and how much of the new head's 0.35 us is VectorE's and how much the order's.
